# Second tile of a retention and MLP kernel: block 6's scalings moved ahead on GpSimd, its v rounded last, and half of one Strassen operand sum moved from GpSimd to VectorE

## The chip, the cores and the metric

The kernel runs on one core of a Trainium2 chip. A core has a matrix engine (TensorE, PE in the profile), VectorE (DVE), ScalarE (ACT), GpSimd (POOL) and SyncE (SP, which here only issues DMAs). Each engine has its own queue and works through it in order; engines wait for each other by semaphores. Operands lie in SBUF, matmul results in PSUM, inputs and outputs in HBM. The metric is the device time of one execution in microseconds (us), lower is better; the time is a median over runs, and one more execution was profiled.

## The reference

```python
# q, k, v: (8 batches, 8 heads, 576 positions, 64)
scores = scale * q @ k^T
ret    = scores * (gamma_h ** (i - j) where i >= j, else 0)
attn   = ret @ v                       # (8, 8, 576, 64)
x      = attn.transpose(0, 2, 1, 3).reshape(4608, 512)
h = x @ w_in                           # (4608, 2048)
g = h * cos(h)
out = g @ w_out                        # (4608, 512)
```

The first part is retention: attention without softmax, whose decay gamma factors into a factor of the query's position and one of the key's. The second is an MLP with the activation h cos h.

## The kernel before, in words

The 4608 tokens are cut into 18 blocks of 256 (`BK`) for the retention and into 9 tiles of 512 (`W`) for the MLP. Tile n of the MLP uses the retention outputs of blocks 2n and 2n + 1, transposed and in bf16, in `xT`. The retention of later blocks is woven into the matmuls of the running tile. The whole order is written out by hand; no planner chooses it.

Block j of the retention goes through these steps. `load` (L133) brings q, k and v by DMAs that SyncE issues, into tiles with three buffers each (`fq`, `fk`, `fv`). `prep(j)` (L217) multiplies q and k by their decay factors and rounds to bf16: four GpSimd instructions, L203, into `qks`. `round_v(j)` (L210) rounds v to bf16: two GpSimd instructions, L214. `turned` (L225) transposes q and k on PE and copies them out of PSUM (L245). `scores` (L287) multiplies them, and two VectorE masks (L341) write `ret`. `sums_of` (L351) makes the running states: PE products (L365), VectorE additions (L412, L416), then a rounding on ScalarE (L425) that must have read the states before the next block's additions overwrite them. `out_own` and `out_carried` (L449, L484) give the block's outputs on PE, from the masked scores and from the states.

For tile n, `mm1` makes h in groups of 1024 columns (L534); ScalarE takes the cosine (L547) and VectorE multiplies (L548) into `gT`. The second matmul, g @ w_out, is done for all tiles but the first by a scheme of seven products in place of eight (`mm2_seven`, L670; `product`, L617; its matmuls are L649). The products are numbered. Products 5, 6, 7 and 3 take as their stationary operand sums of quarters of `gT`, made by `g_sum` (L570, instructions L588): with quarters G(r, c) for token half r and d_ff half c, sum 5 is G10 + G11, sum 6 is sum 5 - G00, sum 7 is G00 - G10, and sum 3 is G01 - sum 6. Each sum has eight slices of 256 columns; slices 0 to 3 are called its first half here, 4 to 7 its second. `g_sum` on VectorE is one instruction for a half, on GpSimd two (two slices each). Without a given engine, sum 3 goes to GpSimd in the second tile and sum 7 to VectorE.

The second tile is n = 1, from about 46 to 82 us. Its h come in eight groups, i = 0 to 7 (L998 to L1039). Behind groups 0 and 1 stand `step`, which runs `prep` and `round_v` for blocks 4 and 5, and the loads of blocks 6 and 7. Behind group 5 stands VectorE's first half of sum 5, and behind group 7 its first half of sum 6. Then `mm2_seven` runs the products in the order 2, 4, 6, 5, 7, 3 (product 1 was made earlier). Ahead of product 6 runs `first_scores` (L1107): the second halves of sums 5 and 6 on VectorE, then on PE the scores of block 4 (`a`) and the state products of blocks 4 and 5, on VectorE the first mask of block 4, its state additions, the second mask, and later the state additions of block 5. Ahead of product 7 runs `next_scores` (L1122): outputs of block 4, scores of block 5 (`b`) and on VectorE its two masks. Ahead of product 3 runs `last_outputs` (L1141): the rest of block 4's outputs, block 5's outputs, which need both masks of block 5, and the transposes of block 6.

So GpSimd's queue in the second tile is: block 4's scalings and v, block 5's scalings and v, the first half of sum 7, block 6's scalings, the second half of sum 7 (held by `gate=six` until VectorE has finished sum 6), the first half of sum 3, block 6's v, the second half of sum 3, and then block 7's scalings and v.

Of the kernel before, what the change touches and what calls it, by code (L numbers as in the profile page):

```python
# [17 lines left out]
def kernel(  # L18
# [9 lines left out]
    nc = tc.nc  # L28
# [13 lines left out]
    E2 = ET // 2  # L42
# [82 lines left out]
    def after(i, gate):  # L125
        tc.add_manual_dep(
            i.ins,
            gate.ins.name,
            mybir.DependencyInfo(mybir.DependencyClass.Sync, mybir.DependencyReason.DATA),
            reason="in this order",  # L130
        )

    def load(j, names="qkv", gate=None):  # L133
        for name in names:
            src = {"q": q, "k": k, "v": v}[name]
            if name == "q" or j < NP_B:
                f = ld.tile([P, H, 2, D], F32, tag="f" + name, name=f"f{name}")
                for p0, p1, t in parts_of(j * BK, BK, 2):
                    b, s0 = divmod(t, S)
                    i = nc.sync.dma_start(  # L140
                        f[p0:p1].rearrange("p h r d -> p h (r d)"),
                        src[b, :, s0 : s0 + 2 * (p1 - p0), :].rearrange(
                            "h (p r) d -> p h (r d)", r=2
                        ),
                    )
                    if gate is not None:
                        after(i, gate)
                        gate = None
            else:
                f = ld.tile([P, 2, H, D], F32, tag="f" + name, name=f"f{name}")  # L150
                for y in range(2):
                    for p0, p1, t in parts_of(j * BK + y * P, P, 1):
                        b, s0 = divmod(t, S)
                        i = nc.sync.dma_start(
                            f[p0:p1, y],
                            src[b, :, s0 : s0 + p1 - p0, :].rearrange("h s d -> s h d"),
                        )
                        if gate is not None:
                            after(i, gate)
                            gate = None  # L160
            tiles["f" + name, j] = f
        return i
# [29 lines left out]
    def scaled(eng, j, name, y):  # L192
        f = tiles["f" + name, j]
        if ("qks", j) not in tiles:
            tiles["qks", j] = nat.tile([P, 2, 2, HG, 2, D], BF16, tag="qks", name="qks")
        dst = tiles["qks", j][:, "qk".index(name), y]
        if name == "q" or j < NP_B:
            src = f[:, :, y, :]
            by = (gq if name == "q" else gkp)[:, j % PERQ, y, :]
        else:  # L200
            src = f[:, y]
            by = gkc[:, (2 * j + y) % PERK, :]
        return eng.tensor_tensor(  # L203
            out=dst.rearrange("p b a d -> p a b d"),
            in0=src.rearrange("p (a b) d -> p a b d", a=2),
            in1=by.rearrange("p (a b) -> p a b", a=2).unsqueeze(3).to_broadcast([P, 2, HG, D]),
            op=ALU.mult,
        )
# [8 lines left out]
    def prep(j, eng_q=nc.gpsimd):  # L217
        for name in "qk":
            for y in range(2):
                scaled(eng_q if name == "q" else nc.gpsimd, j, name, y)  # L220
# [334 lines left out]
    def w_sums(x, e0, e1):  # L555
        if x == 7:
            w_sum[x] = w_quarter(0, 1)
        elif x not in w_sum:
            w_sum[x] = consts.tile([P, E2, N2], BF16, tag=f"ws{x}", name=f"ws{x}")
        a, b = {  # L560
            5: lambda: (w_quarter(0, 1), w_quarter(0, 0)),
            6: lambda: (w_quarter(1, 1), w_sum[5]),
            4: lambda: (w_quarter(1, 0), w_sum[6]),
            7: lambda: (w_quarter(1, 1), w_quarter(0, 1)),
        }[x]()
        nc.vector.tensor_tensor(
            out=w_sum[x][:, e0:e1], in0=a[:, e0:e1], in1=b[:, e0:e1], op=ALU.subtract
        )

    def g_sum(n, x, e0, e1, gate=None, eng=None):  # L570
        gT = tiles["g", n]

        def quarter(r, c):
            return gT[:, c * E2 : (c + 1) * E2, r * 256 : (r + 1) * 256]

        if ("gs", n, x) not in tiles:
            tiles["gs", n, x] = sump.tile([P, E2, 256], BF16, tag=f"gs{x}", name=f"gs{x}")
        a, b, op_ = {
            5: lambda: (quarter(1, 0), quarter(1, 1), ALU.add),
            6: lambda: (tiles["gs", n, 5], quarter(0, 0), ALU.subtract),  # L580
            7: lambda: (quarter(0, 0), quarter(1, 0), ALU.subtract),
            3: lambda: (quarter(0, 1), tiles["gs", n, 6], ALU.subtract),
        }[x]()
        if eng is None:
            eng = nc.gpsimd if x == (7 if n > 1 else 3) else nc.vector
        step = 2 if eng is nc.gpsimd else e1 - e0
        for e in range(e0, e1, step):
            i = eng.tensor_tensor(  # L588
                out=tiles["gs", n, x][:, e : e + step],
                in0=a[:, e : e + step],  # L590
                in1=b[:, e : e + step],
                op=op_,
            )
            if gate is not None:
                after(i, gate)
                gate = None
        return i
# [187 lines left out]
    loaded, prepared = 2, 0  # L785

    def load_next(**kw):
        nonlocal loaded
        if loaded < NB:
            load(loaded, **kw)  # L790
            loaded += 1
# [156 lines left out]
    prepared = 4  # L948
# [27 lines left out]
    def turn_of(n):  # L976
        return "mab" if n % 2 else "amb"
# [8 lines left out]
    def states_and_scores(j, st_bank, sc_bank):  # L986
        add = sums_of(j, st_bank) if st_bank else None
        masks = scores(j, [sc_bank])
        if add:
            add()()  # L990
        for masked in masks:
            masked()
# [3 lines left out]
    for n in range(NT):  # L996
        blocks = blocks_of.get(n) or [(e + k * E2, 0, W) for e in range(0, E2, 2) for k in range(2)]
        for i, (et, c0, cw) in enumerate(blocks):  # L998
            inside = {
                (0, 0): {2: block1_outputs},  # L1000
                (1, 0): {
                    2: lambda: (turned(3, "b", (vec, act)), w_sums(4, 4, E2)),
                    4: lambda: adds.append(sums_of(3, ("n", "st"))()),
                },
                (1, 2): {2: lambda: states_and_scores(3, None, ("n", "st"))},
                (1, 3): {1: lambda: adds.pop()()},
                (1, 4): {2: lambda: (turned(4, ("st", "a"), (act, vec)), w_sums(7, 4, E2))},
                (1, 7): {2: lambda: turned(5, "m", (act, vec))},
                (2, 0): {1: lambda: adds.append(sums_of(6, ("n", "st"))())},
                (2, 1): {1: lambda: adds.pop()()},  # L1010
                (2, 5): {1: lambda: turned(7, ("n", "st"))},
            }.get((n, i), {})
            mm1(n, et, c0, cw, banks_of.get(n, turn_of(n) * 3)[i], inside)
            if (n, i) == (1, 0):
                step(False)
                load_next()
            if (n, i) == (1, 1):
                step(False)
                for r0, ot in stores[3:] + stores[:3]:
                    stored_rows(r0, 0, DM, ot)  # L1020
                load_next()
            if (n, i) == (1, 3):
                w_sums(7, 0, 4)
                mm2_seven(1, {}, None, (1,), lambda: outputs(3, "a"))
            if n:
                sums_after(n, i)
            if n == 2 and i in (2, 4):
                for y in range(2):
                    scaled(nc.gpsimd, 8, "q" if i == 2 else "k", y)
            if (n, i) == (1, 5):  # L1030
                g_sum(n, 7, 0, 4, eng=nc.gpsimd)
                prep(6)
                load_next()
                prepared = 7
            if (n, i) == (2, 6):
                round_v(8)
                prepared = 9
                load_next()
                load_next()  # L1039
# [67 lines left out]
        def first_scores(flush, pend):  # L1107
            g_sum(n, 5, 4, E2)
            six = g_sum(n, 6, 4, E2)
            masks = scores(a, "a")  # L1110
            add_a = sums_of(a, "b")
            add_b = sums_of(b, "m")
            masks[0]()
            add_a()()
            masks[1]()
            g_sum(n, 7, 4, E2, gate=six, eng=nc.gpsimd)
            g_sum(n, 3, 0, 4)
            round_v(6)
            g_sum(n, 3, 4, E2)
            tiles["rounded"] = add_b()  # L1120

        def next_scores(flush, pend):  # L1122
# [93 lines left out]
```

## Time and profile before

| what | value |
|---|---|
| median of 3 runs | 292.85 us (292.78 to 293.01) |
| the profiled execution | 292.24 us |
| its span (first to last instruction) | 290.5 us |
| granted TensorE clock | 1.0 throughout |
| TensorE busy | 281.8 us, 97% |
| VectorE busy | 218.8 us, 75% |
| ScalarE busy | 169.4 us, 58% |
| GpSimd busy | 149.5 us, 51% |

A row of a timeline reads: start and duration in us, engine, line of the kernel, operation, output and inputs by the program's names, shapes, and the count of instructions that the row joins. In square brackets stands how long the engine had been idle before it and what ended that. A row of waits gives the total, the count and the longest. A row of the chain gives start, duration and what the time was spent on. A row of the DMA issues ends with the size and the time from issue to landing. The names: `gs` is a sum of quarters, `gT` the activations, `qks` the scaled q and k, `vb` the rounded v, `ret` the masked scores, `s_all` the states, `o` and `ot` the second matmul's results, `ov` the retention's outputs, `st` the state products.

### The profile page before, as it was taken

How to read it: one execution, taken by the hardware profiler on the slowest of the kernel's cores; microseconds unless marked ns; L12 is line 12 of the kernel's file. 1: busy time of each engine (PE TensorE's matmuls, PEld its weight loads, DVE VectorE, ACT ScalarE, POOL GpSimd, SP SyncE). 2: the span in 40 equal slices, each digit the busy share in tenths (PEclk: the TensorE clock that was granted, in tenths of full speed). 3: DMA queues.
4: the chain of work that ended last, by engine and by line, in shares of the span. 5: the costliest groups of instructions: out<-in, count | busy, mean ns of one | idle time of the engine just before them, and what ended most of it. 6: DMA issues, size and time to landing. Idle time of an engine off the chain costs nothing.

```text
span 290.5 us, 10511 instructions
## 1 busy us (share of the span) xinstructions
PE 281.8 (97%) x4315; PEld 190.7 (66%) x4336; DVE 218.8 (75%) x310; ACT 169.4 (58%) x200; POOL 149.5 (51%) x171
## 2 busy tenths in 40 slices
PE   8999999998999999999999999999999999999994
PEld 3664446887854786478646874687458845874584
DVE  5777768979968877796779776977698669745943
ACT  6756216755577745677467737673767476536620
POOL 7941434779996994369235933494338023002300
PEclk9999999999999999999999999999999999999999
DMA  7999999998998947963893289317501130122013
GB/s 225 269 175 204 255 245 221 239 220 202 231 247 217 256 101 181 244 137 81 186 236 85 46 216 239 85 41 188 142 0 39 38 77 0 34 60 57 0 38 108
DMA packets 103853, 42.62 MB, mean 147 GB/s; under 512 B 68480, under 2 KB 103296, under 8 KB 103808
## 3 DMA queue, kind: packets, MB, share of 16 engines
q1 hardware_dynamic: 99104, 37.37, 52.4%
q0 software_dynamic: 4256, 4.19, 9.0%
q8 instruction: 36, 0.59, 0.8%
q10 hardware_dynamic: 448, 0.39, 0.4%
q14 instruction: 9, 0.07, 0.1%
HBM read 36.70 MB, written 9.44 MB: 159 GB/s over the span
## 4 chain that ended last, share of the span: by engine, by line
PE 91%; DVE 5%; DMA 1%; issue 1%; ACT 1%; DVEq 0%
PE h L534 42%; PE o L649 33%; PE o L1071 4%; PE tr L239 3%; PE ov L449 3%; PE sc L332 2%; DVE ret L312 1%; PE ov L484 1%; DVE gs L588 1%; DMA fk<-in_k_dram 1%; PE st L365 1%; DVE qks L171 1%; DVE gT L548 1%; ACT cosh L547 1%; PE sc L299 0%
## 5 line engine op out<-in xcount | busy, mean ns | idle before, releaser
L534 PE MATMUL h<-xT,w_in_sb 128*128 128x512 bf16 (+1 forms) x640 | 126.7, 353 | 0.8
L548 DVE TENSOR_TENSOR gT<-h,cosh 128x1024 bf16<-128x1024 f32 x72 | 87.9, 1222 | 27.4 <-ACT cosh L547 26.5
L547 ACT ACTIVATE cosh<-h,half_pi 128x1024 f32<-128x1024 f32 x72 | 80.1, 1115 | 38.9 <-PE h L534 38.9
L534 PEld LDWEIGHTS <-w_in_sb 128*128 128x128 bf16 x656 | 63.4, 98 | 58.7 <-issue 0.2
L588 POOL TENSOR_TENSOR gs<-gT 128x512 bf16<-128x512 bf16 x32 | 40.9, 1280 | 98.9 <-DVE gT L548 98.3
L649 PEld LDWEIGHTS <-gs 128*128 128x128 bf16 x528 | 49.5, 98 | 7.2 <-DVE gs L588 1.3
L203 POOL TENSOR_TENSOR qks<-fk,gkc 128x512 bf16<-128x512 f32 x32 | 39.5, 1251 | 5.5 <-DMA fk<-in_k_dram 5.5
L649 PEld LDWEIGHTS <-gT 128*128 128x128 bf16 x384 | 36.6, 98 | 6.1
L678 DVE TENSOR_TENSOR ot<-ot,o 128x512 f32<-128x512 f32 x35 | 23.3, 682 | 20.9 <-ACT ot L682 12.6
L245 ACT COPY qkT<-tr 128x1024 bf16<-128x1024 bf16 x28 | 26.8, 1021 | 13.0 <-PE tr L239 11.0
L203 POOL TENSOR_TENSOR qks<-fq,gq 128x512 bf16<-128x512 f32 x28 | 30.7, 1113 | 3.6 <-DMA fq<-in_q_dram 1.9
L649 PE MATMUL o<-ws,gs 128*128 128x256 bf16 (+1 forms) x264 | 30.6, 269 | 1.0 <-DVE gs L588 1.0
L649 PE MATMUL o<-w_out_sb,gs 128*128 128x256 bf16 (+1 forms) x264 | 30.7, 270 | 0.0
L649 PE MATMUL o<-w_out_sb,gT 128*128 128x256 bf16 x256 | 30.6, 273 | 0.0
L682 ACT COPY ot<-o 128x512 f32<-128x512 f32 x33 | 19.3, 585 | 19.1 <-PE o L649 19.1
L425 ACT CAST sb<-s_all 128x768 bf16<-128x768 f32 (+2 forms) x17 | 15.6, 919 | 16.9 <-DVE s_all L416 16.9
L341 DVE TENSOR_TENSOR ret<-sc,mask_c 128x512 bf16<-128x512 f32 x32 | 20.6, 683 | 6.4 <-PE sc L332 6.4
L214 POOL CAST vb<-fv 128x512 bf16<-128x512 f32 x35 | 21.1, 627 | 7.0 <-DMA fv<-in_v_dram 6.8
L416 DVE TENSOR_TENSOR s_all<-st,s_all 128x256 f32<-128x256 f32 x49 | 20.7, 422 | 1.8 <-ACT sb L425 0.3
L505 ACT CAST xT<-ov 128x1024 bf16<-128x1024 f32 (+1 forms) x16 | 15.2, 959 | 7.4 <-PE ov L484 7.3
L588 DVE TENSOR_TENSOR gs<-gT 128x512 bf16<-128x512 bf16 (+1 forms) x23 | 15.9, 690 | 0.5
L588 DVE TENSOR_TENSOR gs<-gs,gT 128x1024 bf16<-128x1024 bf16 x16 | 15.5, 970 | 0.3
(85 smaller groups left out, 211.9 us busy)
## 6 DMA issues: line engine op xcount, KB each, us to landing
out_dram<-ot SPq DMA_DIRECT2D x68, 128.0 KB, 2.7
fk<-in_k_dram SPq DMA_DIRECT2D x28, 256.0 KB, 5.2
fv<-in_v_dram SPq DMA_DIRECT2D x28, 256.0 KB, 4.2
fq<-in_q_dram SPq DMA_DIRECT2D x12, 512.0 KB, 5.0
w_out_sb<-in_moe_w_out_dram POOLq DMA_DIRECT2D x4, 512.0 KB, 9.6
fq<-in_q_dram SPq DMA_DIRECT2D x4, 384.0 KB, 5.5
fk<-in_k_dram SPq DMA_DIRECT2D x2, 512.0 KB, 4.9
fv<-in_v_dram SPq DMA_DIRECT2D x2, 512.0 KB, 5.9
```

The costliest lines, as they stand in the source:

```text
L203: return eng.tensor_tensor(out=dst.rearrange("p b a d -> p a b d"), in0=src.rearrange("p (a b) d -> p a b d", a=2), in1=by.rearrange("p (a ...
L214: runs[y](vb[:, y], f[:, :, y, :] if j < NP_B else f[:, y])
L245: lambda r=r: evacs[r](tiles["qkT", j][:, :, :, :, r * HP : r * HP + HP], pss[r])
L341: nc.vector.tensor_tensor(out=ret[:, he].rearrange("p b y i -> p (b y) i"), in0=ps[he].rearrange("p b y i -> p (b y) i"), in1=mask_c.unsqu ...
L416: nc.vector.tensor_tensor(out=s32[:, u], in0=ps[c.half][:, c.y], in1=s32[:, u - 1] if u else tiles["run"], op=ALU.add,)
L534: nc.tensor.matmul(ps[:, j, :], lhsT=w_in_sb[:, dg, (et + j) * P : (et + j + 1) * P], rhs=xT[:, dg, c0 : c0 + w], start=dg == 0 and not (i ...
L547: nc.scalar.activation(cosh, ps, ACTF.Sin, bias=half_pi, scale=1.0)
L548: nc.vector.tensor_mul(gT[:, et : et + m, c0 : c0 + w], ps, cosh)
L588: i = eng.tensor_tensor(out=tiles["gs", n, x][:, e : e + step], in0=a[:, e : e + step], in1=b[:, e : e + step], op=op_,)
L649: nc.tensor.matmul(dst[i], lhsT=lhs[:, e, j * P : (j + 1) * P], rhs=rhs[:, e, c0:c1], start=(fresh and e == 0 and (i == 0 or len(parts) > 2)),
L678: return lambda: nc.vector.tensor_tensor(out=out_, in0=in0, in1=in1, op=ALU.add)
L682: held.append(lambda ps=tiles["all", x]: nc.scalar.copy(t, ps))
```

## The change

Four edits in the second tile. `prep(6)` and the load of block 8 move from behind group 5 to behind group 1, so that GpSimd scales block 6 straight behind block 5's v. GpSimd's first half of sum 7 behind group 5 is gone; in `first_scores` VectorE makes it in one instruction, between the second mask of block 4 and the state additions of block 5. The two halves of sum 3 on GpSimd become one call (the same four instructions), and block 6's v is rounded behind all four of them, not between the second and the third.

```diff
@@ behind the groups of h
                 for r0, ot in stores[3:] + stores[:3]:
                     stored_rows(r0, 0, DM, ot)
                 load_next()
+                prep(6)
+                prepared = 7
+                load_next()
             if (n, i) == (1, 3):
...
-            if (n, i) == (1, 5):
-                g_sum(n, 7, 0, 4, eng=nc.gpsimd)
-                prep(6)
-                load_next()
-                prepared = 7
             if (n, i) == (2, 6):
@@ first_scores
             masks[1]()
             g_sum(n, 7, 4, E2, gate=six, eng=nc.gpsimd)
-            g_sum(n, 3, 0, 4)
+            g_sum(n, 3, 0, E2)
             round_v(6)
-            g_sum(n, 3, 4, E2)
+            g_sum(n, 7, 0, 4)
             tiles["rounded"] = add_b()
```

## The prediction

> **What bounds the kernel now.** I read the page first, then TensorE's waits, the chain of waits around the place that the diff touches, and last the order of time on each engine there. The page's first lines:
>
> ```profile
> span 290.5 us, 10511 instructions
> PE 281.8 (97%) x4315; PEld 190.7 (66%) x4336; DVE 218.8 (75%) x310; ACT 169.4 (58%) x200; POOL 149.5 (51%) x171
> ```
>
> TensorE (PE) is busy 97% of the span, so only its few pauses can be won. The waits of PE between 63 and 82 us, which is the end of the second tile, have one row, and the chain of waits passes through the same place:
>
> ```profile
> PE o L649 <- DVE gs L588: 1.0, 1, 1.0
> ```
>
> ```profile
> 68.73 2.69 DVE gs L588 x2
> ```
>
> The chain lies on sums of VectorE (DVE), two in this row and the one at 71.45 below: the first half of the sixth product's sum, made behind the last block, then the second halves of the fifth's and the sixth's. PE in order of time (start, duration, count of matmuls at the row's end):
>
> ```profile
> 67.91 1.91 PE L649 MATMUL o<-ws,gT 128*128 128x256 bf16 x16
> ...
> 70.87 1.05 PE L649 MATMUL o<-ws,gs 128*128 128x256 bf16 x8
> 72.92 2.79 PE L649 MATMUL o<-ws,gs 128*128 128x256 bf16 x24 [1.00 <-DVE gs L588]
> 75.64 0.32 PE L449 MATMUL ov<-ret,vb 64*64 64x64 bf16 x16
> 75.79 0.43 PE L332 MATMUL sc<-qkT 64*64 64x64 bf16 x32
> 76.15 1.92 PE L649 MATMUL o<-w_out_sb,gs 128*128 128x256 bf16 x16
> ...
> 78.15 0.36 PE L484 MATMUL ov<-qkT,sb 64*64 64x64 bf16 x24
> 78.53 0.32 PE L449 MATMUL ov<-ret,vb 64*64 64x64 bf16 x16
> ```
>
> The sixth product stops after 8 matmuls. The 24 behind the stop step at about (75.64 - 72.92 - 0.1) / 24 = 0.109 us, so the ninth was due at 70.87 + 8 x 0.109 = 71.74 and the stop costs 72.92 - 71.74 = 1.18 us (the row shows less because the eighth matmul's modelled tail counts as busy). Why the sums are late stands in VectorE's and GpSimd's (POOL's) orders of time:
>
> ```profile
> 64.59 0.69 DVE L588 TENSOR_TENSOR gs<-gT 128x1024 bf16<-128x1024 bf16 x1
> 65.20 1.22 DVE L548 TENSOR_TENSOR gT<-h,cosh 128x1024 bf16<-128x1024 f32 x1
> 66.43 0.69 DVE L245 COPY qkT<-tr 128x1024 bf16<-128x1024 bf16 x1
> 67.51 1.23 DVE L548 TENSOR_TENSOR gT<-h,cosh 128x1024 bf16<-128x1024 f32 x1 [0.39 <-ACT cosh L547]
> 68.65 1.32 DVE L588 TENSOR_TENSOR gs<-gs,gT 128x1024 bf16<-128x1024 bf16 x1
> 69.89 1.52 DVE L588 TENSOR_TENSOR gs<-gT 128x1024 bf16<-128x1024 bf16 x1
> 71.45 1.42 DVE L588 TENSOR_TENSOR gs<-gs,gT 128x1024 bf16<-128x1024 bf16 x1
> 72.78 0.68 DVE L341 TENSOR_TENSOR ret<-sc,mask_c 128x512 bf16<-128x512 f32 x1
> ...
> 74.50 0.68 DVE L341 TENSOR_TENSOR ret<-sc,mask_c 128x512 bf16<-128x512 f32 x1
> 75.48 1.80 DVE L416 TENSOR_TENSOR s_all<-st,s_all 128x256 f32<-128x256 f32 x4 [0.30 <-ACT sb L425]
> 77.20 1.28 DVE L341 TENSOR_TENSOR ret<-sc,mask_c 128x512 bf16<-128x512 f32 x2
> ```
>
> ```profile
> 61.94 1.28 POOL L214 CAST vb<-fv 128x512 bf16<-128x512 f32 x2
> 64.64 2.77 POOL L588 TENSOR_TENSOR gs<-gT 128x512 bf16<-128x512 bf16 x2 [1.42 <-DVE gT L548]
> 67.38 2.04 POOL L203 TENSOR_TENSOR qks<-fq,gq 128x512 bf16<-128x512 f32 x2
> ...
> 72.94 2.27 POOL L588 TENSOR_TENSOR gs<-gT 128x512 bf16<-128x512 bf16 x2 [0.63 <-DVE gs L588]
> 75.17 2.27 POOL L588 TENSOR_TENSOR gs<-gT,gs 128x512 bf16<-128x512 bf16 x2
> 77.38 1.17 POOL L214 CAST vb<-fv 128x512 bf16<-128x512 f32 x2
> 78.51 2.27 POOL L588 TENSOR_TENSOR gs<-gT,gs 128x512 bf16<-128x512 bf16 x2
> ```
>
> and, from narrower windows, the two scalings of block 6's k, one by one:
>
> ```profile
> 69.38 1.49 POOL L203 TENSOR_TENSOR qks<-fk,gkc 128x512 bf16<-128x512 f32 x1
> ```
>
> ```profile
> 70.83 1.49 POOL L203 TENSOR_TENSOR qks<-fk,gkc 128x512 bf16<-128x512 f32 x1
> ```
>
> Read the two engines against each other. The same VectorE sum takes 0.69 us at 64.59 and 1.32, 1.52, 1.42 us later. The one at 68.65 ends at 69.97, 0.55 after GpSimd's scaling ends at 69.42; the next GpSimd scaling takes 1.49 in place of some 1.02 (2.04 for two), and the next VectorE sum ends 0.54 after it (70.87 to 71.41); so again to 72.32 and 72.87. The two take turns, whole instructions at a time. At 64.59 VectorE came first, and it was GpSimd that took 0.5 us longer (2.77 for two, against 2.27 at 72.94). The masks (L341) and the products with the cosine (L548) keep 0.68 and 1.22 beside running GpSimd instructions: those read PSUM for one input, the sums read SBUF for both. The Trainium skill says this in "SBUF — State Buffer", section "Who interferes with whom": a VectorE instruction with two SBUF inputs contends with a GpSimd instruction that reads SBUF, and whichever issues first holds the port while the other fully blocks; the trace agrees, 0.69 against 1.32 to 1.52 us.
>
> **The change part by part.**
>
> Block 6's scalings (four GpSimd instructions) move ahead, straight behind block 5's last rounding, which ends at 61.94 + 1.28 = 63.22. Their data decide the start. SyncE's issues and their times to landing, each from its own narrow window:
>
> ```profile
> 57.81 1.48 SPq L140 DMA_DIRECT2D fq<-in_q_dram  x2
> 59.35 3.94 SPq L154 DMA_DIRECT2D fk<-in_k_dram  x3
> ```
>
> ```profile
> fq<-in_q_dram SPq DMA_DIRECT2D x1, 128.0 KB, 5.5
> ```
>
> ```profile
> fk<-in_k_dram SPq DMA_DIRECT2D x1, 128.0 KB, 3.2
> ```
>
> These are the last part of q, issued at 58.7, and the last of k, issued at 62.6: q is complete at 58.7 + 5.5 = 64.2, k at 62.6 + 3.2 = 65.8. Four scalings alone take 2 x 2.04 = 4.1 us. So they start at about 64.3, give way once for 0.5 us to VectorE's sum of 64.59, and end at 64.3 + 4.1 + 0.5 = 68.9 in place of 72.32. The load of block 8 that moves with them keeps its place in SyncE's queue (behind block 7's; nothing else is issued between the two places), and the tiles that it overwrites are block 5's, free at 63.2: cost nothing.
>
> Price of the earlier place: the VectorE sum of 64.59 now finds GpSimd running and waits until about 65.35 + 0.55 = 65.9, which is 0.6 late. Behind it the product with the cosine ends at 67.05, the copy L245 at 67.75 and the last product at 67.67 + 1.23 = 68.9, 0.17 late. PE's fourth product needs the copy's bank at 67.91: it is covered with 0.16 to spare. If VectorE had to wait a further 0.3 there, PE would lose 0.15.
>
> The three sums then run free of GpSimd: start 68.82, about 0.62 + 0.7 + 0.7 each, end at 70.84 (call this T) in place of 72.87. PE wants it at 71.74, so the whole 1.18 us goes, with 0.9 to spare.
>
> Half of the seventh product's sum leaves GpSimd (2.77 us at 64.64, off the path) and returns on VectorE as one 0.69 us instruction behind the second mask. By the rows of before, the masks and the state additions between them take from 0.08 before T to 74.50 + 0.68 = 75.18, or T + 2.31, so the new sum asks at T + 2.24. GpSimd's sums of 1.11 us start to start begin at T + 0.07 (72.94), so the second ends at T + 2.34 and the third would be issued at T + 2.30 (75.17). VectorE asks in front of the third: it waits little or nothing, and ends at T + 2.95 = 73.8. If it loses by those 0.06 us it waits for the third as well and ends near T + 4.0 = 74.85. The seventh product starts at 76.15 - 1.18 = 74.97, so both ends are in time.
>
> Behind the new sum on VectorE stand the state additions of block 5 and its two masks, which PE needs before the row of 78.53. The additions waited 0.30 for ScalarE's rounding until 75.48 = T + 2.61, so part of the new sum lies in that pause. They would start at T + 2.87 and the masks end 78.48 - 75.48 = 3.0 later: 76.7, or 77.8 if the port is lost. PE wants them at 78.53 - 1.18 - 0.09 = 77.26; the 0.09 is what PE pauses there now (the row of 78.15 ends 0.02 ahead of 78.53, where back-to-back rows overlap by 0.07). So the pause goes too (gain 1.27 in all), or comes back as 0.55.
>
> Block 6's v is rounded behind all of the third sum. GpSimd's work from T is then 2.27 + 2 x 2.27 + 1.17 plus 0.5 of giving way, ending at 79.3; the third product's sum is whole at 78.2 in place of 78.51 + 2.27 = 80.78. That is 2.6 earlier for a PE that comes 1.27 earlier, and PE did not wait for it before. The rounded v, at 79.3 in place of 77.38 + 1.17 = 78.55, is first read by PE in the third tile, behind the whole third product, which alone is 16 matmuls of 0.109: hidden by that product. If that cover went, it would cost up to the 0.75 that it is later and the 1.27 that PE is earlier. No other instruction is added; from the third tile on PE has no wait on another engine of over 0.2 us, so what is won here is kept.
>
> Sum: the profiled execution took 292.24 us (span 290.5 and 1.7 around it); minus 1.18 and 0.09 is 290.97. The median of the runs is 292.85, 0.61 above the profiled one; minus the same 1.27, rounded down to 1.25, it is 291.6.
>
> **The rivals.**
>
> The port is lost. The new sum comes behind GpSimd's third sum, the masks of block 5 end at 77.8, and PE takes them up at 77.8 in place of 78.53: gain 0.7, 292.1. For it: the margin is 0.06 us. Against it: the order of before puts VectorE in front. The rule of the Trainium skill quoted above gives the same 292.1 for the worse order, since the new sum has two SBUF inputs and GpSimd's sums read SBUF too.
>
> The change does not clear the way. If block 6's k lands later, or the scalings start late, two of them still stand among the three sums and T is about 71.7 to 72: PE's stop shrinks to nothing or 0.3, but the masks of block 5 end at T + 5.9 = 77.6 to 77.9, or later if the port is lost: gain 0 to 0.6, about 292.6. For it: the k parts land only 3 us ahead of the first of those sums, on queues that are busy. Against it: nothing ahead of 63 us is moved.
>
> Slower: VectorE's queue becomes what PE waits for. If T stays near 72.9, because the scalings slip by 4 us, nothing is won at the sums, and the added sum pushes the masks of block 5 by 0.4 to 1.5, past PE's 78.53: 0.4 to 1.5 slower, 293.6 in the middle. It decides from T later than 78.48 - 5.9 = 72.6, or than 71.5 with the port lost. Against it: that needs 0.7 us of slip and a lost port, or 1.8 us of slip alone.
>
> **How the numbers follow.** Port kept 0.50 (291.6, range 291.3 to 291.9), port lost 0.22 (292.1), way not cleared 0.15 (292.6), slower 0.13 (293.6). The last two share the smallest effects. Runs spread by 0.23 us and profile and median differ by 0.6, so 0.2%, 0.6 us, is about what can be told from no change: faster means below 292.26, slower above 293.44. The first case and most of the second lie below: 0.71; same takes the edge of the second, the third and a part of the last: 0.19; slower 0.10. The range reaches from the first case's lower end, less 0.1 for the spread, over the third case: 291.2 to 293.0.
>
> **What would show it.** GpSimd's scalings of block 6 between about 64 and 69 us, and the VectorE sum of 64.59 lengthened to about 1.3; then three sums of 0.69 each, and no PE wait on them; the new sum directly behind the second mask, at 0.7 (port kept) or 1.8 (lost); the row that answers to 78.53 at about 77.3, or 77.8; the third tile's products the same. Wrong would be: scalings that still run at 69 to 72; a PE wait at the fourth or seventh product; a later tile that gives the microsecond back.

## The result and the profile after

The changed kernel takes 291.2 us (median of 6 runs, 290.92 to 291.54), the kernel before 292.9 us in the same comparison (292.45 to 293.24): ratio 0.9943, 95% interval 0.9930 to 0.9956. It is faster by 1.7 us, between 1.3 and 2.0 by the interval. The forecast was 291.6, a gain of 1.25, with a range of 291.2 to 293.0: the measured time lies on the lower end of the range.

PE no longer has a row of waits for the sums. The row with which the third product began before the change, and then PE's order of time after it, the same columns as before:

```profile
79.86 1.92 PE L649 MATMUL o<-w_out_sb,gs 128*128 128x256 bf16 x16
```

```profile
71.21 3.67 PE L649 MATMUL o<-ws,gs 128*128 128x256 bf16 x32
74.80 0.32 PE L449 MATMUL ov<-ret,vb 64*64 64x64 bf16 x16
74.95 0.43 PE L332 MATMUL sc<-qkT 64*64 64x64 bf16 x32
75.31 1.92 PE L649 MATMUL o<-w_out_sb,gs 128*128 128x256 bf16 x16
77.16 0.32 PE L449 MATMUL ov<-ret,vb 64*64 64x64 bf16 x16
77.31 0.36 PE L484 MATMUL ov<-qkT,sb 64*64 64x64 bf16 x24
77.50 0.33 PE L449 MATMUL ov<-ret,vb 64*64 64x64 bf16 x16
...
78.85 1.92 PE L649 MATMUL o<-w_out_sb,gs 128*128 128x256 bf16 x16
```

The sixth and fifth products run as one row of 32 matmuls; before they were 8 and, after the stop, 24. From the first matmul of the sixth product to the first of the third it is 78.85 - 71.21 = 7.64 us, where it was 79.86 - 70.87 = 8.99: 1.35 less. Two pieces make it up. The stop of 1.18 is gone: the sixth and fifth products take 74.80 - 71.21 = 3.59 us, where they took, stop included, 75.64 - 70.87 = 4.77. So is the pause ahead of block 5's outputs: from the row of L484 with 24 matmuls to the next row it is 0.19 us now (77.31 to 77.50), 0.38 before (78.15 to 78.53). The two are 1.37; the rows behind take 0.02 longer. The profile begins the sixth product 0.34 later than that of before, so clock times of the two are compared with that shift.

VectorE and GpSimd after the change:

```profile
64.93 0.69 DVE L588 TENSOR_TENSOR gs<-gT 128x1024 bf16<-128x1024 bf16 x1
...
68.99 1.09 DVE L588 TENSOR_TENSOR gs<-gs,gT 128x1024 bf16<-128x1024 bf16 x1
70.00 0.68 DVE L588 TENSOR_TENSOR gs<-gT 128x1024 bf16<-128x1024 bf16 x1
70.71 0.69 DVE L588 TENSOR_TENSOR gs<-gs,gT 128x1024 bf16<-128x1024 bf16 x1
...
73.04 0.68 DVE L341 TENSOR_TENSOR ret<-sc,mask_c 128x512 bf16<-128x512 f32 x1
73.64 0.68 DVE L588 TENSOR_TENSOR gs<-gT 128x1024 bf16<-128x1024 bf16 x1
74.24 1.79 DVE L416 TENSOR_TENSOR s_all<-st,s_all 128x256 f32<-128x256 f32 x4
75.94 1.28 DVE L341 TENSOR_TENSOR ret<-sc,mask_c 128x512 bf16<-128x512 f32 x2
```

```profile
65.44 2.09 POOL L203 TENSOR_TENSOR qks<-fq,gq 128x512 bf16<-128x512 f32 x2 [1.23 <-DMA fq<-in_q_dram]
67.49 2.04 POOL L203 TENSOR_TENSOR qks<-fk,gkc 128x512 bf16<-128x512 f32 x2
71.48 2.27 POOL L588 TENSOR_TENSOR gs<-gT 128x512 bf16<-128x512 bf16 x2 [1.96 <-PE st L365]
73.70 4.98 POOL L588 TENSOR_TENSOR gs<-gT,gs 128x512 bf16<-128x512 bf16 x4
78.62 1.17 POOL L214 CAST vb<-fv 128x512 bf16<-128x512 f32 x2
```

Block 6's scalings end at 69.53. Only the first of the three sums still meets one (1.09); the other two take 0.68 and 0.69. The third ends at 71.40; PE, which begins the product at 71.21, wants it eight matmuls, 0.87 us, later, at 72.08. The sum that the change adds to VectorE stands at 73.64 with 0.68. It got its turn at once, 0.06 ahead of GpSimd's next sums at 73.70. Their four instructions take 4.98 in place of twice 2.27, so it is GpSimd that gives way.

### The profile page after: what moved, and what is told of

It reads as the page before. It is cut to its first block, busy times and chain, and to the rows that moved or that the text cites. A ratio compares the mean times of both kernels' runs of the same rounds, so it can differ in the third digit from the quotient of the medians.

```text
span 289.8 us, 10531 instructions
## 1 busy us (share of the span) xinstructions
PE 283.2 (98%) x4336; PEld 190.3 (66%) x4336; DVE 217.7 (75%) x311; ACT 169.5 (58%) x200; POOL 146.0 (50%) x169
## 4 chain that ended last, share of the span: by engine, by line
PE 92%; DMA 4%; POOL 1%; SPq 0%; issue 0%; ACT 0%; DVE 0%; POOLq 0%
PE h L534 43%; PE o L649 35%; PE o L1069 5%; PE tr L239 3%; PE ov L449 2%; DMA w_in_sb<-in_moe_w_in_dram 2%; DMA fv<-in_v_dram 2%; PE sc L332 2%; PE ov L484 1%; PE st L365 1%; POOL qks L203 1%; SPq L140 0%; POOL w_in_sb L814 0%; POOL vb L214 0%; ACT ot L682 0%
## 5 line engine op out<-in xcount | busy, mean ns | idle before, releaser
L588 POOL TENSOR_TENSOR gs<-gT 128x512 bf16<-128x512 bf16 x30 | 38.1, 1270 | 99.2 <-DVE gT L548 97.2
L203 POOL TENSOR_TENSOR qks<-fk,gkc 128x512 bf16<-128x512 f32 x32 | 38.5, 1222 | 5.7 <-DMA fk<-in_k_dram 5.7
L649 PE MATMUL o<-ws,gT 128*128 128x256 bf16 x128 | 15.3, 273 | 0.0
```

The lines of the kernel that those rows point to most:

```text
L203: return eng.tensor_tensor(out=dst.rearrange("p b a d -> p a b d"), in0=src.rearrange("p (a b) d -> p a b d", a=2), in1=by.rearrange("p (a ...
L588: i = eng.tensor_tensor(out=tiles["gs", n, x][:, e : e + step], in0=a[:, e : e + step], in1=b[:, e : e + step], op=op_,)
L649: nc.tensor.matmul(dst[i], lhsT=lhs[:, e, j * P : (j + 1) * P], rhs=rhs[:, e, c0:c1], start=(fresh and e == 0 and (i == 0 or len(parts) > 2)),
```

## The experiments

Two explanations were to be told apart. By the first, the port theory, the gain is that VectorE's three sums, which read both inputs from SBUF, no longer meet GpSimd instructions that read SBUF. By the rivals it comes from another part of the change (the earlier place of the scalings, the later v), or from GpSimd's shorter queue as such. The stretch named above, from the first matmul of the sixth product to the first of the third, is the measure that isolates the place; the table gives it, from one profiled execution, for every kernel beside the median of its runs. The first two rows are one comparison; the other kernels were timed in two groups of runs beside the kernel before, whose medians there were 292.89 and 292.83. Diffs are against the changed kernel unless it says before.

| kernel | stretch, us | median, us | ratio to before, 95% interval |
|---|---|---|---|
| before | 8.99 | 292.9 | |
| changed | 7.64 | 291.2 | 0.9943 (0.9930 to 0.9956) |
| `place` | 7.64 | 291.25 | 0.9937 (0.9918 to 0.9956) |
| `vback` | 7.64 | 291.02 | 0.9932 (0.9911 to 0.9953) |
| `nosum` | 7.64 | 291.52 | 0.9950 (0.9933 to 0.9967) |
| `sumpool` | 8.27 | 292.74 | 0.9985 (0.9969 to 1.0000) |
| `dread` | 8.64 | 293.22 | 1.0008 (0.9992 to 1.0024) |
| `sumlate` | 8.75 | 292.74 | 0.9996 (0.9978 to 1.0015) |
| `vonly` | 9.00 | 292.78 | 0.9994 (0.9979 to 1.0009) |
| `dwrite` | 7.64, and 0.62 in the third product | 292.3 | 0.9985 (0.9970 to 1.0000) |

The stretch does not give every median. Counted from 292.9, the stretches of `sumpool` and `dread` would make it 292.2 and 292.55; their medians lie 0.6 and 0.7 above that, with executions from 291.73 to 293.99 and from 291.92 to 294.16, and no profile shows where. So the readings below rest on the stretch; the medians only part the kernels that keep the gain (291.52 and less) from the others (292.3 and more).

### The place in the text alone

```diff
             if (n, i) == (1, 1):
...
-                prep(6)
-                prepared = 7
-                load_next()
...
+            if (n, i) == (1, 5):
+                prep(6)
+                load_next()
+                prepared = 7
```

> The changed kernel, with block 6's scalings and block 8's load written back behind group 5; only the first half of sum 7 is gone from GpSimd there. GpSimd's and SyncE's queues hold the same instructions in the same order either way. Port theory (the gain is that VectorE's three sums no longer meet GpSimd): the move in the text is nothing by itself, what counts is that GpSimd's half of sum 7 no longer stands ahead of the scalings; 291.2 us, within 0.3 of the changed kernel, scalings of block 6 from about 65.4 us. Rival (the earlier place in the text is what gains): most of the 1.7 us is lost, above 292.3.

It took 291.25 us. The move in the text is nothing by itself: once GpSimd's half of sum 7 is gone, the queues of GpSimd and SyncE hold the same instructions in the same order, and the scalings follow block 5's v either way. In this run q landed earlier, and the price that the prediction put on an early start shows:

```profile
63.69 2.04 POOL L203 TENSOR_TENSOR qks<-fq,gq 128x512 bf16<-128x512 f32 x2 [1.07 <-DMA fq<-in_q_dram]
65.70 2.49 POOL L203 TENSOR_TENSOR qks<-fk,gkc 128x512 bf16<-128x512 f32 x2
```

```profile
64.93 1.36 DVE L588 TENSOR_TENSOR gs<-gT 128x1024 bf16<-128x1024 bf16 x1
...
69.07 0.68 DVE L588 TENSOR_TENSOR gs<-gs,gT 128x1024 bf16<-128x1024 bf16 x1
69.67 0.68 DVE L588 TENSOR_TENSOR gs<-gT 128x1024 bf16<-128x1024 bf16 x1
70.38 0.69 DVE L588 TENSOR_TENSOR gs<-gs,gT 128x1024 bf16<-128x1024 bf16 x1
```

The sum behind group 5 meets the scalings (1.36), and all three later sums are free. PE's stretch is the same 7.64, so the late products and the late copy behind that sum were covered. The cover is thin: in `sumlate` below that sum took 1.58, and the fourth product began 1.80 us after the second, where it is 1.75 here.

### Half of sum 7 stays on GpSimd, behind the scalings

Against the kernel before:

```diff
             if (n, i) == (1, 5):
-                g_sum(n, 7, 0, 4, eng=nc.gpsimd)
                 prep(6)
+                g_sum(n, 7, 0, 4, eng=nc.gpsimd)
                 load_next()
```

> The kernel before, with block 6's scalings ahead of GpSimd's half of sum 7, which stays on GpSimd; v in its old place. Port theory: the scalings are out of the way by about 69.5 us, but the two GpSimd sums then run from there to about 72 and read SBUF too, so VectorE's second and third sum still wait for them, the third sum ends at 72.0 to 72.9 (71.4 in the changed kernel, 72.9 before), PE's stop at the sixth product is 0.3 to 1.2 us, and the time 292.0 to 292.9. Rival (the block 6 scalings had to come early, for the load or the transposes): 291.2 as in the changed kernel.

```profile
68.22 2.71 POOL L588 TENSOR_TENSOR gs<-gT 128x512 bf16<-128x512 bf16 x2
```

```profile
68.72 1.20 DVE L588 TENSOR_TENSOR gs<-gs,gT 128x1024 bf16<-128x1024 bf16 x1
69.84 1.64 DVE L588 TENSOR_TENSOR gs<-gT 128x1024 bf16<-128x1024 bf16 x1
71.52 0.69 DVE L588 TENSOR_TENSOR gs<-gs,gT 128x1024 bf16<-128x1024 bf16 x1
```

```profile
72.26 2.79 PE L649 MATMUL o<-ws,gs 128*128 128x256 bf16 x24 [0.28 <-DVE gs L588]
```

The scalings were over even earlier than in the changed kernel (68.26 against 69.53), and 292.74 us came of it: the two GpSimd sums take the scalings' place beside VectorE's first two sums (1.20 and 1.64), the third ends at 72.21, and PE still stops. Early scalings alone bring about half: the stretch is 0.72 shorter than before, of the 1.35, and the median 0.15 us, with an interval that reaches no change.

### The later v alone, and the change without it

Against the kernel before:

```diff
-            g_sum(n, 3, 0, 4)
+            g_sum(n, 3, 0, E2)
             round_v(6)
-            g_sum(n, 3, 4, E2)
```

> The kernel before, with nothing but block 6's v rounded behind all four GpSimd instructions of sum 3. Port theory: PE waited for neither, so no change, 292.9 within 0.3, and PE's stop of 1.0 us at the sixth product stays. Rival (the third product's sum was the hidden limit): 0.3 to 0.7 faster, 292.2 to 292.6.

292.78 us, and PE's stop is there as before:

```profile
73.07 2.79 PE L649 MATMUL o<-ws,gs 128*128 128x256 bf16 x24 [1.01 <-DVE gs L588]
```

The reverse, the changed kernel with v between the halves of sum 3 again:

```diff
-            g_sum(n, 3, 0, E2)
+            g_sum(n, 3, 0, 4)
             round_v(6)
+            g_sum(n, 3, 4, E2)
             g_sum(n, 7, 0, 4)
```

> The changed kernel, with block 6's v back between the halves of sum 3. Port theory: the last instruction of sum 3 ends 1.2 us later, at about 79.8, and PE wants it at about 80.1: 0.3 to spare, 291.2 within 0.3. Rival (with PE earlier the third product's sum becomes the limit): a PE wait of 0.2 to 0.6 inside the third product, 291.5 to 291.8.

291.02 us. In this profile the second half of sum 3 ends at 77.29 + 2.27 = 79.56, and the third product, begun at 78.61, had no wait:

```profile
78.61 1.92 PE L649 MATMUL o<-w_out_sb,gs 128*128 128x256 bf16 x16
```

```profile
77.29 2.27 POOL L588 TENSOR_TENSOR gs<-gT,gs 128x512 bf16<-128x512 bf16 x2
```

So the later v neither gives nor takes anything here.

### GpSimd kept busy beside VectorE's sums, reading and not reading

Two GpSimd sums more behind the scalings, into a spare tile (the line that allocates it is left out here, and in the next diff):

```diff
                 prep(6)
+                for _ in range(2):
+                    nc.gpsimd.tensor_tensor(out=spare[:, 0], in0=w_in_sb[:, 0, :512], in1=w_in_sb[:, 1, :512], op=ALU.add)
                 prepared = 7
```

> The changed kernel, with two more GpSimd sums behind block 6's scalings, of two columns of w_in into a spare tile that nobody reads; all else the same, the output too. Port theory: they run from about 69.5 to 72 us and read SBUF, so VectorE's second and third sum meet them; the third sum ends at 72.4 to 72.9 in place of 71.4, PE stops 0.3 to 0.8 us at the sixth product, and block 5's masks come late by a few tenths as well: 291.7 to 292.7 us. Rival (the gain came from GpSimd's shorter queue ahead of sums 7 and 3, not from VectorE's sums): GpSimd's later sums start about 0.4 to 1.4 us later and nothing waits for them, 291.2.

```profile
68.53 2.71 POOL L1025 TENSOR_TENSOR spare<-w_in_sb 128x512 bf16<-128x512 bf16 x2
```

```profile
68.86 1.36 DVE L589 TENSOR_TENSOR gs<-gs,gT 128x1024 bf16<-128x1024 bf16 x1
70.15 1.64 DVE L589 TENSOR_TENSOR gs<-gT 128x1024 bf16<-128x1024 bf16 x1
71.82 0.69 DVE L589 TENSOR_TENSOR gs<-gs,gT 128x1024 bf16<-128x1024 bf16 x1
```

```profile
72.57 2.79 PE L650 MATMUL o<-ws,gs 128*128 128x256 bf16 x24 [0.44 <-DVE gs L589]
...
78.39 0.32 PE L450 MATMUL ov<-ret,vb 64*64 64x64 bf16 x16 [0.23 <-DVE ret L342]
```

Both losses come back, a stop of 0.62 us at the sixth product (72.57, where the ninth matmul was due at 71.08 + 0.87 = 71.95) and a pause of 0.40 at block 5's masks (0.59 from the row of 77.80 to that of 78.39, less the 0.19 of the changed kernel): the stretch is 1.00 longer than in the changed kernel. The median, 293.22, lies above the expected 292.7, and 2.0 above the changed kernel's. The second microsecond is not in the stretch, and its cause is open: the profiled execution took 292.33, so its trace can't show what the slower ones lost.

Nine GpSimd fills at the same place, which read nothing:

```diff
                 prep(6)
+                for _ in range(9):
+                    nc.gpsimd.memset(spare[:, 0], 0.0)
                 prepared = 7
```

> The changed kernel, with nine GpSimd fills of a spare tile at the same place as the two sums of the run before, some 2 us in all by the 0.21 us of a fill at the start of the kernel; they read nothing. Port theory with reading as its condition: VectorE's sums keep 0.69 us beside them, no stop at the sixth product, 291.2 within 0.3. Rival (any GpSimd instruction blocks VectorE's sums): sums of 0.8 us and more, and up to 1 us slower than the changed kernel.

```profile
69.28 5.17 POOL L1025 MEMSET spare<- 128x512 bf16 x9
```

```profile
69.42 0.68 DVE L589 TENSOR_TENSOR gs<-gs,gT 128x1024 bf16<-128x1024 bf16 x1
70.02 0.69 DVE L589 TENSOR_TENSOR gs<-gT 128x1024 bf16<-128x1024 bf16 x1
70.73 0.69 DVE L589 TENSOR_TENSOR gs<-gs,gT 128x1024 bf16<-128x1024 bf16 x1
```

```profile
79.28 1.48 PE L650 MATMUL o<-w_out_sb,gs 128*128 128x256 bf16 x12
81.21 0.50 PE L650 MATMUL o<-w_out_sb,gs 128*128 128x256 bf16 x3 [0.45 <-POOL gs L589]
```

The sums keep 0.68 and 0.69 us beside a GpSimd that fills without a pause, and the sixth product does not stop. Beside the two sums of `dread`, which read SBUF, they took 1.36 and 1.64: it is the reading that blocks. The Trainium skill says the same in "SBUF — State Buffer", section "Who interferes with whom": a VectorE instruction with two SBUF inputs contends with a GpSimd instruction that reads SBUF, not with one that only writes.

The expected 291.2 was missed, at 292.3. A fill takes 5.17 / 9 = 0.57 us, not 0.21; the 0.21 was that of a fill of 128 x 128, a quarter of the elements. So sums 7 and 3 on GpSimd began at 74.42 in place of 71.48, 2.5 us later against the sixth product's start, and now the third product waited for sum 3. Its thirteenth matmul was due at 79.28 + 12 x 0.109 = 80.59 and began at 81.21: 0.62 us (the row shows less, as at the sixth product). The rest of the 1.1 is not placed. The rival's mechanism, a GpSimd queue that is too long, exists, then, but it needs that queue some 2.5 us longer than in the changed kernel.

### The price of the added VectorE sum, and of its place

Left out, with the seventh product reading the first half of sum 6 in its place (the output is not the reference's):

```diff
-            g_sum(n, 7, 0, 4)
             tiles["rounded"] = add_b()
...
-                lhsT=lhs[:, e, j * P : (j + 1) * P],
+                lhsT=(tiles["gs", n, 6] if (n, x) == (1, 7) and e < 4 else lhs)[:, e, j * P : (j + 1) * P],
```

> The changed kernel without the first half of sum 7: left out, and the seventh product of the second tile reads the first half of sum 6 in its place, so the output is not the reference's. It prices the VectorE sum that the change adds. Theory of the prediction: it lies in VectorE's pause and ahead of a PE that comes later anyway, so without it nothing changes: 291.2 within 0.3, with the masks of block 5 ending about 0.4 us earlier. Rival (the added sum costs something on the path): 0.2 to 0.6 faster than the changed kernel.

291.52 us, just above the expected 291.5, and the stretch is the same 7.64: the added sum costs nothing on the path. Counted from the end of the third sum, block 5's masks end only 0.05 earlier than in the changed kernel (5.77 us behind it against 5.82), not the expected 0.4. Without the added sum VectorE pauses again for ScalarE's rounding, as before the change:

```profile
74.51 1.80 DVE L416 TENSOR_TENSOR s_all<-st,s_all 128x256 f32<-128x256 f32 x4 [0.30 <-ACT sb L425]
```

One place later in VectorE's queue:

```diff
-            g_sum(n, 7, 0, 4)
             tiles["rounded"] = add_b()
+            g_sum(n, 7, 0, 4)
```

> The changed kernel, with the first half of sum 7 on VectorE behind block 5's state additions, one place later than in the change. Theory of the prediction: it is then asked for at about 75.7 us, between GpSimd's sums, and ends at 76.4 to 77.0 while the seventh product is due at 75.3; PE stops there for 1.1 to 1.7 us: 292.2 to 292.9. Rival (PE has more room than worked out): 291.2 to 291.6.

```profile
75.45 0.78 DVE L588 TENSOR_TENSOR gs<-gT 128x1024 bf16<-128x1024 bf16 x1
```

```profile
76.29 1.92 PE L649 MATMUL o<-w_out_sb,gs 128*128 128x256 bf16 x16 [1.05 <-DVE gs L588]
```

292.74 us: the seventh product stops for 1.05 us, and the stretch gives back 1.11 of the 1.35. The sum itself waited for GpSimd only 0.1 (0.78); it is the four state additions ahead of it (1.80), and VectorE's pause of 0.30 before them, that make it late.

### Where the rest of the difference lies

The medians differ by 1.7 us, the stretch by 1.35. Both kernels were profiled once more, unchanged, in turn on one chip, one execution each.

> The kernel before, unchanged, profiled once more, to see how much of the difference of the medians (1.7 us) lies outside the second tile. If all of the gain is the stop and the pause, the stretch from the first matmul of the sixth product to the first of the third is 8.99 us again, and what lies ahead of and behind it differs from the first profile by a few tenths in either direction. If the change also gains elsewhere, the stretches outside are longer here than in the changed kernel, each time.

> The changed kernel, unchanged, profiled once more. The stretch from the sixth product to the third is 7.64 us again, 1.35 shorter than before; outside it the same few tenths in either direction as in the kernel before. The VectorE sum behind group 5 takes 0.69 to 1.6 us, by when block 6's q lands, and PE waits for nothing of it.

The kernel before, and then the changed one (the last row of the first ends with the window that it was read from):

```profile
70.94 1.05 PE L649 MATMUL o<-ws,gs 128*128 128x256 bf16 x8
...
79.94 1.26 PE L649 MATMUL o<-w_out_sb,gs 128*128 128x256 bf16 x10
```

```profile
70.92 3.67 PE L649 MATMUL o<-ws,gs 128*128 128x256 bf16 x32
...
78.56 1.92 PE L649 MATMUL o<-w_out_sb,gs 128*128 128x256 bf16 x16
```

The executions took 292.30 and 290.91 us, spans 290.6 and 289.2. The stretch is 9.00 and 7.64, so 1.36 of the 1.39 lie in it, and the stretch ahead of it is the same within 0.02. In this pair the whole gain is the place that the change touches. In the first pair the stretch differs by 1.35, but the profiled executions only by 0.70 (292.24 and 291.54). The further 0.3 of the medians is not placed; 1.36 is inside their interval of 1.3 to 2.0. Other profiles scatter by as much elsewhere: the first profile of the changed kernel began the sixth product 0.34 later than that of before, `nosum` 1.23 later, with the same instructions ahead of it.

## Why the prediction was right

**The bound and its cause** held: three sums that read SBUF twice, one by one behind GpSimd's scalings. `dread` brings the stop back by reading alone, `dwrite` does not by filling, and `sumpool` shows that GpSimd's sums at that time do it as its scalings did. The prediction lets the move in the text bring the scalings ahead; `place` shows that leaving out GpSimd's half of sum 7 does that alone.

**The stop of 1.18** was right: 1.18 is gone, with 0.68 to spare (71.40 against 72.08) where 0.9 was worked out. The difference is q's landing. It was put at 64.2 and the first scaling at 64.3; in the first profile after the change the scalings began at 65.44, in the second at 64.40, in `place` at 63.69. With the late landing the sum behind group 5 is free and the first of the three sums meets the last scaling; with the early one it is the other way round. Both were affordable, as the working said of the copy with its 0.16 to spare; `sumlate`, with the longest wait there, lost 0.05.

**The pause at block 5's masks** was mis-sized: taken as 0.09, it measured 0.19 (0.38 less 0.19 from one row to the next). The working let the row of 78.15 overlap the next by 0.07 when PE doesn't pause; after the change, without a pause, it is 0.17 (77.31 + 0.36 = 77.67 against 77.50). With it the sum is 1.37, not 1.27 rounded to 1.25, where the stretch measured 1.35 and 1.36.

**The number** is less sure than the mechanism. The median came out 0.4 below the forecast, at the very end of the range. 0.1 of that is the pause. The other 0.3 is placed by no profile, so it is luck that it did not carry the time out of the range.

**The port** was the open point, with 0.06 us between the two cases. With T for the end of the third sum, 71.40, the new sum was at T + 2.24 (73.64), as worked out, and got its turn; the masks of block 5 ended at 77.22 and PE took them up at 77.50. The margin was small but steady: VectorE was 0.06 or 0.07 us ahead in both profiles of the changed kernel and in `place`, `vback` and `dread`, as VectorE's queue and GpSimd's held sums both start from T. The order was lost in no profile of these instructions, so the 292.1 of that rival stays untried. The rival in which the way is not cleared did not occur in the changed kernel, but `sumpool` is its mechanism, and 0.63 us of stretch its price. The slower rival needed T later than 72.6, if the port is kept, with the added sum in the way; `dread` comes nearest, with T at 72.51, or 72.30 by the clock of before. Its stretch is still 0.35 shorter than before and its median the same (ratio 1.0008), so that rival was not reached either.

**The terms put at nothing** were nothing in the stretch: the place of the load (`place`), the later v (`vonly`, `vback`), the added sum (`nosum`).

## What to carry to other kernels

In these traces a VectorE sum with both inputs in SBUF took 0.68 us alone or beside GpSimd fills, and up to 1.64 where it had to wait for a GpSimd instruction that reads SBUF, while VectorE's masks and its products with the cosine, with one input in PSUM, kept some 0.68 and 1.22. So plan the two engines' SBUF-reading work as one queue, and put GpSimd's reading work beside VectorE's PSUM work. An instruction taken off an engine that is half idle can pay, when it moves what stands behind it out of the way of another engine's critical run. Where it is put back decides as much: in front of the state additions it was free, behind them it cost 1.1 us.

## What the runs showed of the hardware that was not expected

A GpSimd fill of 128 x 512 bf16 took 0.57 us, about what the casts of as many elements take in these profiles (1.17 for two), though it reads nothing. Where both queues were backed up with such instructions, the turn changed at every instruction: in `sumpool` GpSimd's two sums end at 69.37 and 70.93 and VectorE's at 69.92 and 71.48, each 0.55 behind, and neither engine got two in a row there.
